# Attention and slot experts in one kernel: zero products, exponentials copied to row groups, logits and row sums moved

## The chip, the cores and the metric

The kernel runs on one core of one Trainium2 chip. The metric is the device time of one execution in microseconds. Six runs of the kernel before gave 151.49 to 153.0 us, with a median of 152.21 us.

## The reference, cut to what matters

Attention over 4 batches, 8 heads, 768 positions and 64 columns a head, with two kinds of mask; its output, as 3072 rows of 512 columns, goes into a layer of 8 experts with 4 slots each. The logits are exponentiated and normalised twice: over the rows (what goes into a slot) and over the 32 slots (what comes back out).

```python
mask = np.where(retr[0, :, 0, 0, None, None], full_mask, stream_mask)
scores = np.where(mask[None, :, :, :], scores, -1000000000.0)
a = np.exp(scores - np.max(scores, axis=-1, keepdims=True))
a = a / (np.sum(a, axis=-1, keepdims=True) + 1e-09)
x = np.matmul(a, v)                  # then (B*S, H*D)
...
logits = x @ phi                     # (3072, 32)
d = np.exp(logits - logits.max(0, keepdims=True))
d /= d.sum(0, keepdims=True) + 1e-09
slot_input = (d.T @ x).reshape(E, S_per_e, D)
for e in range(E):
    h = np.maximum(slot_input[e] @ w1[e], 0.0)
    slot_out[e] = h @ w2[e]
c = np.exp(logits - logits.max(1, keepdims=True))
c /= c.sum(1, keepdims=True) + 1e-09
return c @ slot_out                  # (3072, 512)
```

## The kernel before, in words

The kernel leaves out both subtractions of a maximum, since the values are small, so one exponential of the logits serves both normalisations.

Attention goes through 16 pairs of heads (n), four pairs to a batch (bt counts them, one pair late: bt = 0 to 3 for the pairs 4b+4 to 4b+7). A pair has six groups (g), each a piece of the causal triangle. The order is written out by hand: the loop over n and g issues, on every engine, the score products (qk, L114), the exponentials on ACT (L119, L123), the masks on DVE (L133, L136), the transposes of the next pair's q, k and v (L78) with their evacuations (L91), the products with v (pvmm, L149), the normalisation (norm, L160 and L162) and the transpose of the pair before for the logits (x_transpose, L170, evac_x, L176). Each engine works through its own instructions in this order.

For each batch, three steps follow one or two pairs behind: token_logits multiplies the transposed attention output with phi (L188); exp_tokens takes the exponential (L199) into elg, which has the 32 slots four times side by side, in four groups of columns; exp_slots multiplies elg with a permutation (L205), which brings the slots onto 128 partitions, four copies of each, in expT. dispatch (L219) multiplies the first group of columns of elg with the attention output, to the slots' input. row_sums (L239, L240) sums expT over the slots for each row and takes the reciprocal, which only the last step (piece, L592 and L594) uses. These small results share a PSUM pool of two buffers, "tr", with the transposes.

warm (L62) issues products of zeros into a PSUM tile that is not read. They stand at L333 (20, while the first loads arrive), at L377 (4, after the first transposes), and in the tail.

GpSimd's queue has the loads that also turn float32 into bfloat16: q, k and v of pair n + 3 (L69) and one expert weight of 1024 KB in most pairs (L273), all remaining weights in pair 13 (L275). A load waits until its buffer is free. The queue works in order. Only the first q and k and small inputs go by SP and ACT, and the output goes by SP (L595).

After the last pair comes the tail: logits and exponentials of the last batch, the slots' input (L231), the experts' first layer (L520), transposes, and the second layer (layer2, L548) expert by expert. The weights of experts 6 and 7 for it come in two column halves. slot_cols (L574) scales a half, and piece (L589) makes the output: first the left halves of batches 0 and 1, then their right halves, then whole rows of batches 2 and 3. ACT and DVE evacuate the output products alternately.

Of the kernel before, what the change touches and what calls it, by code (L numbers as in the profile page):

```python
# [14 lines left out]
ACT = mybir.ActivationFunctionType  # L15
# [4 lines left out]
P = 128  # L20
# [15 lines left out]
class Attn:  # L36
# [152 lines left out]
                                      start=first, stop=True, skip_group_check=True)  # L189
                first = False  # L190

    def exp_tokens(self, b, c, groups=range(4)):

        if b not in self.elg:
            self.elg[b] = self.small.tile([P, 6, 4, 32], BF16, tag="eb", name="elg", bufs=1)
        e = self.lg[b, c][:, :, :]
        e = bass.AP(tensor=e.tensor, offset=e.offset,
                    ap=[e.ap[0], e.ap[1], [0, len(groups)], e.ap[2]])
        self.nc.scalar.activation(self.elg[b][:, 3 * c:3 * c + 3, groups[0]:groups[-1] + 1, :], e, ACT.Exp)  # L199

    def exp_slots(self, b, c, eng=None):

# [41 lines left out]
def kernel(  # L244
# [13 lines left out]
    nc = tc.nc  # L258
    B, H, S, D = q.shape
# [11 lines left out]
    def w_load(i, c0=0, cl=DM):  # L271
        if i < NE:
            nc.gpsimd.dma_start(w1s[i], moe_w1[i].rearrange("(di do) f -> di do f", do=4))  # L273
        else:
            nc.gpsimd.dma_start(w2s[i - NE][:, :, c0:c0 + cl],  # L275
                                moe_w2[i - NE].rearrange("(fi fo) d -> fi fo d", fo=8)[:, :, c0:c0 + cl])
# [20 lines left out]
    with ExitStack() as actx:  # L297
# [20 lines left out]
        at = Attn(nc, tc, actx, q, k, v, env)  # L318
# [11 lines left out]
        at.zeros = asing.tile([P, 256], BF16, name="zeros")  # L330
        at.waste = at.pvp.tile([P, 256], F32, tag="pv1", name="waste")
        nc.vector.memset(at.zeros, 0.0)
        at.warm(20)  # L333
        nc.gpsimd.memset(ident, 1.0)
        nc.gpsimd.affine_select(ident, ident, pattern=[[-1, P]], compare_op=ALU.is_equal,
                                fill=0.0, base=0, channel_multiplier=1)
# [37 lines left out]
        cast("k", 1, hi, nc.vector)  # L374
        at.transpose(0, "q")
        at.transpose(0, "k")
        at.warm(4)  # L377
        at.evac(0, "q")
        at.evac(0, "k")

# [4 lines left out]
        def head_mask(h):  # L385
            for c0, c1, r in ((0, 256, r0), (256, 640, r1)):
                nc.vector.tensor_scalar(msk[:, h, c0:c1], level[:, c0:c1], r[:, h:h + 1], 2.0,  # L387
                                        op0=ALU.add, op1=ALU.is_ge)

        for n in range(NP):  # L390
            if n + 3 < NP:
                at.load(n + 3)
            for _ in range(len(w_order) if n == 13 else 0 if n % 4 == 3 else 1):
                if w_order:
                    w_load(*w_order.pop(0))
            if n == 1:

                nc.gpsimd.memset(sum4, 1.0)
                for g in range(4):
                    nc.gpsimd.affine_select(sum4[32 * g:32 * (g + 1)], sum4[32 * g:32 * (g + 1)],  # L400
                                            pattern=[[-1, ES]], compare_op=ALU.is_equal,
                                            fill=0.0, base=0, channel_multiplier=1)
                phf = at.small.tile([P, 4, ES], F32, tag="eb", name="phf", bufs=1)
                nc.sync.dma_start(phf, moe_phi.rearrange("(do di) s -> di do s", di=P))
            for g in range(NG):
                at.qk(n, g)
                last = n == NP - 1

                b, bt = (n - 4) // 4, (n - 4) % 4 if n >= 4 else 0
                if g == 0:  # L410
                    if n == 0:
                        at.transpose(0, "v")
                        head_mask(0)
                        at.evac(0, "v")
                        head_mask(1)


                        nc.vector.tensor_scalar(fb0, r0, 1.0, 30000.0, op0=ALU.subtract, op1=ALU.mult)
                        nc.vector.tensor_scalar(fb1, r1, 1.0, 30000.0, op0=ALU.subtract, op1=ALU.mult)
                    else:  # L420
                        at.pvmm(n - 1, 4)
                        at.v_blocks(n)
                        at.evac_blocks(n)
                    at.mask(n, 0)
                elif g == 1:
                    if n:
                        at.pvmm(n - 1, 5)
                    else:
                        at.v_blocks(n)
                        at.evac_blocks(n)  # L430
                    if bt == 1:
                        at.token_logits(b, 0)
                        at.exp_tokens(b, 0)
                    elif bt == 3:
                        at.dispatch(b, slot_bf if last else None)
                    if n:
                        at.norm(n - 1, 1)
                elif g == 2:
                    if not last:
                        at.transpose(n + 1, "q")  # L440
                    at.pvmm(n, 0)
                    at.mask(n, 1)
                    if not last:
                        at.evac(n + 1, "q")
                elif g == 3:
                    if not last:
                        at.transpose(n + 1, "k")
                    at.pvmm(n, 1)
                    at.mask(n, 2)
                    if not last:  # L450
                        at.evac(n + 1, "k")
                elif g == 4:
                    if not last:
                        at.transpose(n + 1, "v")
                    at.pvmm(n, 2)
                    if bt == 1:
                        at.token_logits(b, 1)
                        at.exp_tokens(b, 1)
                    if bt == 3:
                        at.row_sums(b)  # L460
                    if not last:
                        at.evac(n + 1, "v")
                    if 1 <= bt <= 2:
                        at.exp_slots(b, bt - 1)
                elif g == 5:
                    if n:
                        at.x_transpose(n - 1)
                    at.pvmm(n, 3)
                    if n:
                        at.evac_x(n - 1)  # L470
                    at.norm(n, 0)
                if (n, g) in MASK_AT:
                    head_mask(MASK_AT[n, g])
                if n == 2 and g == 0:
                    nc.vector.tensor_copy(phi, phf)
                if n == 3 and 2 <= g:
                    gg = g - 2
                    for e4 in range(2):
                        s0 = SPE * (4 * e4 + gg)
                        nc.vector.reduce_sum(emask[32 * gg:32 * (gg + 1), e4:e4 + 1],  # L480
                                             sum4[32 * gg:32 * (gg + 1), s0:s0 + SPE], axis=AX.X)
        n, b = NP - 1, B - 1
# [13 lines left out]
        at.waste = at.pvp.tile([P, 256], F32, tag="pv0", name="waste")  # L496
        at.warm(2)
        at.token_logits(b, 0, range(3, 4))
        at.exp_tokens(b, 0, range(1))
        at.warm(4)  # L500
        at.x_transpose(n, range(3, 6))
        at.evac_x(n, range(3, 6))
        at.slots_in(sip, b, range(3))
        at.token_logits(b, 1, range(3, 4))
        at.exp_tokens(b, 1, range(1))
        for c in range(2):
            at.exp_tokens(b, c, range(1, 4))
        at.warm(2)
        at.slots_in(sip, b, range(3, 6))
        nc.vector.tensor_copy(siT, sip)  # L510
# [33 lines left out]
        def layer2(e, c0=0, cl=DM):  # L544
            e4, g = e // 4, e % 4
            for fo in range(8):
                r = fo % 4
                nc.tensor.matmul(sp[32 * r:32 * (r + 1), c0:c0 + cl], hT[e4][:, fo, 32 * g:32 * (g + 1)],  # L548
                                 w2s[e][:, fo, c0:c0 + cl], start=(e == 0 and fo < 4),
                                 stop=(e == NE - 1 and fo >= 4), skip_group_check=True)  # L550
# [16 lines left out]
        h_transpose(1, 1)  # L567
        for e in range(2, NE - 2):
            layer2(e)
        at.row_sums(B - 1)  # L570

        def slot_cols(c):

# [6 lines left out]
        def piece(b, r, m, c0=0, cl=DM):  # L580

            er = expT[:, b, :].rearrange("p (t r) -> p r t", r=6)
            ov = out[b * S:(b + 1) * S, :].rearrange("(p r) d -> p r d", r=6)
            ot, o = ots[2 * b + r // 3], r % 3
            for i in range(m):
                k = count[0] = count[0] + 1
                pool, tag = ((at.scp, "sc"), (at.trp, "tr"))[k % 2]
                op = pool.tile([P, DM], F32, tag=tag, name="op")
                nc.tensor.matmul(op[:, :cl], er[:, r + i, :], slot_out[:, c0:c0 + cl], start=True, stop=True)  # L589
                rr = rrow[:, b, r + i:r + i + 1]  # L590
                if k % 2:
                    nc.scalar.activation(ot[:, o + i, c0:c0 + cl], op[:, :cl], ACT.Copy, scale=rr)  # L592
                else:
                    nc.vector.tensor_scalar_mul(ot[:, o + i, c0:c0 + cl], op[:, :cl], rr)  # L594
            nc.sync.dma_start(ov[:, r:r + m, c0:c0 + cl], ot[:, o:o + m, c0:c0 + cl])  # L595
# [4 lines left out]
        slot_cols(0)  # L600
        for b, r, m in ((0, 0, 1), (0, 1, 2), (0, 3, 3), (1, 0, 3), (1, 3, 3)):
            piece(b, r, m, 0, HALF)
        for e in (NE - 2, NE - 1):
            layer2(e, HALF, HALF)
        slot_cols(1)
# [40 lines left out]
```

The softmax here doesn't subtract the row's maximum and nothing guards it: scores larger than these inputs give would overflow.

## Time and profile before

One profiled execution had a span of 149.8 us and a time of 151.49 us, which is the fastest of the six runs; what lies around the span is 1.7 us.

| | before |
|---|---|
| median of 6 runs | 152.21 us |
| profiled execution, its own time | 151.49 us |
| its span | 149.8 us |
| PE busy | 127.2 us (85%) |
| DVE busy | 115.9 us (77%) |
| ACT busy | 114.2 us (76%) |
| GpSimd busy | 42.9 us (29%) |
| read from HBM, written | 52.50 MB, 6.29 MB |

The busy times are sums over the whole span. The attention loop lasts to about 112 us, the tail's products to 126 us; the last loads land at 132.6 us and the last output at 147.8 us. In the lists below, a line begins with the time at which it starts and its length in us; PE is TensorE, DVE VectorE, ACT ScalarE, POOL GpSimd; a name ending in q is that engine's queue. In brackets stands how long the engine was idle before, and what ended the idle time.

### The profile page before, as it was taken

The numbers are of one execution on the slowest core, as the hardware profiler recorded it, in microseconds if no ns is written. First come the engines' busy times: TensorE is split into PE (matmuls) and PEld (weight loads), VectorE is DVE, ScalarE is ACT, GpSimd is POOL, SyncE is SP. The second block draws the span as 40 slices with busy tenths as digits, with TensorE's granted clock in tenths as the row PEclk, the third lists the DMA queues.
The fourth block names the chain that finished last, engine by engine and source line by source line (L and its number), as shares of the span: only waits on it lengthen the run. The fifth ranks groups of instructions, "written<-read, shape, count | busy, mean of one in ns | idle before, by whom it ended". The sixth has DMA issues, their size and how long they took to land.

```text
span 149.8 us, 5539 instructions
## 1 busy us (share of the span) xinstructions
PE 127.2 (85%) x2372; PEld 85.0 (57%) x2372; DVE 115.9 (77%) x287; ACT 114.2 (76%) x183; POOL 42.9 (29%) x77
## 2 busy tenths in 40 slices
PE   7679899998999999999999999999968997739500
PEld 5446566665776666676666667766556453424100
DVE  6399999899897998989799898979965251528800
ACT  3287989998998998999899889989982431738600
POOL 7865524160541515055141332632000000000000
PEclk9999999999999999999999999999999999996985
DMA  4899999999999999999999999999999999999994
GB/s 119 170 209 205 231 191 222 202 229 196 204 228 195 229 194 222 204 201 225 201 226 199 215 210 200 225 214 221 217 214 214 203 194 199 198 340 319 392 415 203
DMA packets 20663, 33.31 MB, mean 222 GB/s; under 512 B 1952, under 2 KB 17952, under 8 KB 18848
## 3 DMA queue, kind: packets, MB, share of 16 engines
q0 software_dynamic: 15744, 25.83, 94.3%
q1 hardware_dynamic: 4688, 6.76, 12.9%
q10 hardware_dynamic: 208, 0.39, 0.9%
q8 instruction: 18, 0.29, 0.7%
q14 instruction: 5, 0.04, 0.1%
HBM read 52.50 MB, written 6.29 MB: 393 GB/s over the span
## 4 chain that ended last, share of the span: by engine, by line
DMA 34%; DVE 30%; PE 15%; ACT 7%; issue 6%; POOL 2%; DVEq 0%; POOLq 0%; ACTq 0%
DMA w<-in_moe_w_dram 20%; DMA vr<-in_v_dram 10%; DVE xb L162 6%; DVE pT L136 5%; PE pv L149 4%; DVE pT L133 4%; ACT pT L123 4%; DMA w<-in_q_dram 3%; DVE vb L103 3%; PE sc L114 3%; DVE xT L176 3%; PE tpx L170 2%; PE op L589 2%; POOL w L275 2%; DVE msk L387 2%
## 5 line engine op out<-in xcount | busy, mean ns | idle before, releaser
L123 ACT ACTIVATE pT<-sc,fb 128x512 bf16<-128x512 f32 (+1 forms) x96 | 52.2, 621 | 3.5 <-PE sc L114 3.1
L119 ACT ACTIVATE pT<-sc 128x1024 bf16<-128x1024 f32 (+1 forms) x48 | 44.6, 953 | 4.1 <-PE sc L114 3.2
L149 PE MATMUL pv<-vb,pT 128*128 128x65 bf16 x672 | 36.9, 194 | 4.3 <-DVE pT L133 2.3
L114 PE MATMUL sc<-qT,kT 64*128 64x256 bf16 (+3 forms) x320 | 35.0, 281 | 0.3
L149 PEld LDWEIGHTS <-pT 128*128 128x128 bf16 x672 | 26.3, 97 | 15.4 <-issue 6.7
L136 DVE TENSOR_TENSOR pT<-pT,msk 128x1024 bf16<-128x1024 bf16 (+1 forms) x32 | 19.8, 618 | 0.0
L162 DVE TENSOR_TENSOR xb<-pv,rs 128x384 bf16<-128x384 f32 x32 | 17.8, 558 | 1.1
L69 POOL DMA_DIRECT2D qr<-in_q_dram x15 | 9.6, 639 | 27.3 <-PE sc L114 12.7
L114 PEld LDWEIGHTS <-kT 64*128 64x128 bf16 x320 | 10.6, 94 | 7.6 <-issue 1.3
L594 DVE TENSOR_SCALAR w<-op,rrow 128x256 f32<-128x256 f32 (+1 forms) x18 | 9.3, 568 | 6.2 <-PE op L589 6.2
L176 DVE COPY xT<-tpx 128x768 bf16<-128x768 bf16 (+1 forms) x17 | 9.1, 533 | 4.2 <-PE tpx L170 4.1
L69 POOL DMA_DIRECT2D vr<-in_v_dram x16 | 10.4, 647 | 6.7 <-PE tpv L78 4.5
L69 POOL DMA_DIRECT2D kr<-in_k_dram x15 | 9.5, 636 | 5.8 <-issue 1.8
L133 DVE TENSOR_TENSOR pT<-pT,msk 128x1024 bf16<-128x1024 bf16 x16 | 10.9, 682 | 0.0
L275 POOL DMA_DIRECT2D w<-in_moe_w_dram x10 | 6.8, 679 | 13.9 <-DMA w<-in_moe_w_dram 11.8
L589 PE MATMUL op<-slot_out,expT 128*128 128x256 bf16 (+1 forms) x36 | 8.7, 351 | 1.8 <-ACT slot_out L574 1.1
L592 ACT ACTIVATE w<-op,rrow 128x256 f32<-128x256 f32 (+1 forms) x18 | 8.9, 542 | 1.2 <-PE op L589 0.9
L78 PE MATMUL tpq<-ident,qr 96*64 96x96 bf16 x256 | 8.7, 209 | 1.2 <-DVE qr L368 1.2
L91 DVE COPY kT<-tpk 128x768 bf16<-128x768 bf16 x16 | 8.8, 552 | 0.5 <-PE tpk L78 0.5
L170 PE MATMUL tpx<-ident,xb 128*128 128x128 bf16 x96 | 8.2, 220 | 0.9 <-ACT elg L199 0.7
L103 DVE COPY vb<-tpb 128x768 bf16<-128x768 bf16 x16 | 8.9, 557 | 0.0
L91 DVE COPY vT<-tpv 128x768 bf16<-128x768 bf16 x16 | 8.8, 548 | 0.0
(86 smaller groups left out, 158.0 us busy)
## 6 DMA issues: line engine op xcount, KB each, us to landing
w<-in_moe_w_dram POOLq DMA_DIRECT2D x14, 1024.0 KB, 15.4
vr<-in_v_dram POOLq DMA_DIRECT2D x16, 192.0 KB, 11.3
out_dram<-w SPq DMA_DIRECT2D x4, 768.0 KB, 5.6
qr<-in_q_dram POOLq DMA_DIRECT2D x15, 192.0 KB, 11.7
kr<-in_k_dram POOLq DMA_DIRECT2D x15, 192.0 KB, 11.4
out_dram<-w SPq DMA_DIRECT2D x6, 384.0 KB, 4.3
w<-in_moe_w_dram POOLq DMA_DIRECT2D x4, 512.0 KB, 30.5
out_dram<-w SPq DMA_DIRECT2D x2, 256.0 KB, 3.6
```

The source lines that it names most:

```text
L69: self.nc.gpsimd.dma_start(t[:96], self.src[w][b, h:h + 2].rearrange("h (p s) d -> p h (s d)", s=8))
L91: self.nc.vector.tensor_copy(o, i)
L103: self.nc.vector.tensor_copy(self.vbufs[n % 2][:, :, :, :64], tp.rearrange("p (j h d) -> p h j d", j=6, h=2))
L114: nc.tensor.matmul(sc[:, hh, c:c + ni * P], kT[po:po + 64, j * P:(j + 1) * P], qT[po:po + 64, i0 * P:(i0 + ni) * P], start=True, stop=True)
L119: nc.scalar.activation(pT[:, :, :L], sc[:, :, :L], ACT.Exp, scale=self.scale)
L123: nc.scalar.activation(pT[:, hh, :L], sc[:, hh, :L], ACT.Exp, scale=self.scale, bias=fb[:, h + hh:h + hh + 1])
L133: nc.vector.tensor_mul(v, v, m)
L136: nc.vector.tensor_mul(pT[:, :, :L], pT[:, :, :L], self.msk[:, h:h + 2, c:c + L])
L149: self.nc.tensor.matmul(self.pv[n, lo][:, hh, i % 3, :], pT[:, hh, o:o + P], vb[:, hh, j, :65], start=first, stop=True, skip_group_check=True)
L162: nc.vector.tensor_mul(xo, pv[:, :, :, :64], rs.to_broadcast([P, 2, 3, 64]))
L176: self.nc.vector.tensor_copy(self.xT[n // 4][:, n % 4, c], self.tp.pop(("x", n))[:, c])
L589: nc.tensor.matmul(op[:, :cl], er[:, r + i, :], slot_out[:, c0:c0 + cl], start=True, stop=True)
```

## The change

The change has four parts. First, more products of zeros: 27 in place of 20 at the start, 6 in place of 4 after the first transposes, 3 after the transposes of the first v, and 4 at the end of each of the groups 0, 1 and 2 of pair 0. Second, exp_tokens takes the exponential into the first group of columns only, and another engine copies that to the other three: GpSimd for batches 0 and 1, DVE for batches 2 and 3. Third, the logits and exponentials of a batch move from groups 1 and 4 of their pair to the ends of groups 0 and 3, and the two exp_slots move from group 4 of the pairs with bt = 1 and 2 to groups 1 and 4 of the pair with bt = 2. Fourth, the row sums leave the attention loop: those of batches 0 and 1 come before the second layer of the last two experts, those of batches 2 and 3 after the first half of the output pieces.

```diff
-    def exp_tokens(self, b, c, groups=range(4)):
+    def exp_tokens(self, b, c, eng):
 
         if b not in self.elg:
             self.elg[b] = self.small.tile([P, 6, 4, 32], BF16, tag="eb", name="elg", bufs=1)
-        e = self.lg[b, c][:, :, :]
-        e = bass.AP(tensor=e.tensor, offset=e.offset,
-                    ap=[e.ap[0], e.ap[1], [0, len(groups)], e.ap[2]])
-        self.nc.scalar.activation(self.elg[b][:, 3 * c:3 * c + 3, groups[0]:groups[-1] + 1, :], e, ACT.Exp)
+        e = self.elg[b][:, 3 * c:3 * c + 3]
+        self.nc.scalar.activation(e[:, :, 0, :], self.lg[b, c], ACT.Exp)
+        eng.tensor_copy(e[:, :, 1:, :], e[:, :, :1, :].to_broadcast([P, 3, 3, 32]))
...
-        at.warm(20)
+        at.warm(27)
...
-        at.warm(4)
+        at.warm(6)
...
                     if n == 0:
                         at.transpose(0, "v")
+                        at.warm(3)
                         head_mask(0)
...
-                    if bt == 1:
-                        at.token_logits(b, 0)
-                        at.exp_tokens(b, 0)
+                    if bt == 2:
+                        at.exp_slots(b, 0)
                     elif bt == 3:
                         at.dispatch(b, slot_bf if last else None)
...
-                    if bt == 1:
-                        at.token_logits(b, 1)
-                        at.exp_tokens(b, 1)
-                    if bt == 3:
-                        at.row_sums(b)
                     if not last:
                         at.evac(n + 1, "v")
-                    if 1 <= bt <= 2:
-                        at.exp_slots(b, bt - 1)
+                    if bt == 2:
+                        at.exp_slots(b, 1)
...
+                if n == 0 and g < 3:
+                    at.warm(4)
+                if bt == 1 and g in (0, 3):
+                    at.token_logits(b, g // 3)
+                    at.exp_tokens(b, g // 3, nc.vector if b == B - 2 else nc.gpsimd)
...
-        at.exp_tokens(b, 0, range(1))
+        at.exp_tokens(b, 0, nc.vector)
...
-        at.exp_tokens(b, 1, range(1))
-        for c in range(2):
-            at.exp_tokens(b, c, range(1, 4))
+        at.exp_tokens(b, 1, nc.vector)
...
-        at.row_sums(B - 1)
+        for b in range(2):
+            at.row_sums(b)
...
         for b, r, m in ((0, 0, 1), (0, 1, 2), (0, 3, 3), (1, 0, 3), (1, 3, 3)):
             piece(b, r, m, 0, HALF)
+        for b in range(2, B):
+            at.row_sums(b)
         for e in (NE - 2, NE - 1):
             layer2(e, HALF, HALF)
         slot_cols(1)
```

## The prediction

> **What bounds the kernel now.** I read the page's slices first, because a busy share per engine hides which engine is never idle.
>
> ```profile
> DMA  4899999999999999999999999999999999999994
> GB/s 119 170 209 205 231 191 222 202 229 196 204 228 195 229 194 222 204 201 225 201 226 199 215 210 200 225 214 221 217 214 214 203 194 199 198 340 319 392 415 203
> ```
>
> PE, DVE and ACT each reach nine tenths in most slices up to 112 us, but only the DMA engines are full in every slice from the third (7.5 us) to the one before last. The GB/s row counts bytes at the destination. Up to 132 us nearly all of it is float32 read and bfloat16 written, so 200 to 230 there are 400 to 460 read. The page's queue part gives GpSimd's queue q0 25.83 MB written, 51.7 MB read; its packets in the trace run from 4.8 to 132.6 us, so 51.7/127.8 = 404 GB/s over the whole stretch. That is the rate of the end as well, where only output is written (399 to 430 GB/s from 141 to 147 us). A stream with the same rate through all stages of the computation is not paced by it.
>
> Then the chain of waits in order of time:
>
> ```profile
> 42.55 0.48 ACT elg L199
> ...
> 45.89 0.55 ACT elg L199
> ...
> 59.08 0.31 PE rp L239 x6
> 59.41 0.21 DVE rrow L240
> ...
> 79.00 15.51 DMA vr<-in_v_dram
> 94.50 0.28 issue
> ...
> 102.56 30.32 DMA w<-in_moe_w_dram
> 132.92 0.43 PE sp L548 x8
> ```
>
> It runs over the compute engines up to 79 us and over DMA from there. Read literally, the computation released the load of vr at 79.00. But this load has 192 KB, 0.9 us at 210 GB/s, and it took 15.51 us: it stood behind 14.6 us of other loads. Issued sooner it would have stood longer. The GpSimd timeline shows the same from the issuing side:
>
> ```profile
> 41.24 0.56 POOL L273 DMA_DIRECT2D w<-in_moe_w_dram  x1 [0.18 <-issue]
> 43.09 0.64 POOL L69 DMA_DIRECT2D qr<-in_q_dram  x1 [1.29 <-DMA kr<-in_k_dram]
> 44.22 0.64 POOL L69 DMA_DIRECT2D kr<-in_k_dram  x1 [0.49 <-PE tpk L78]
> 45.36 0.63 POOL L69 DMA_DIRECT2D vr<-in_v_dram  x1 [0.50 <-PE tpv L78]
> 49.08 0.56 POOL L273 DMA_DIRECT2D w<-in_moe_w_dram  x1 [3.09 <-DMA w<-in_moe_w_dram]
> ```
>
> Issued minus landed, worked out from these times and the 1024 KB and 192 KB of the issue table, the queue never holds less than 1.68 MB (8 us) after 11 us. Last, the timeline of the tail, where the weights meet the computation:
>
> ```profile
> 125.51 0.44 PE L239 MATMUL rp<-quarter,expT 128*128 128x1 bf16 x6
> ...
> 127.42 0.40 PE L548 MATMUL sp<-w,hT 128*32 128x256 bf16 x8 [1.14 <-DMA w<-in_moe_w_dram]
> ...
> 129.20 13.50 SPq L595 DMA_DIRECT2D out_dram<-w  x14
> ...
> 130.78 0.40 PE L548 MATMUL sp<-w,hT 128*32 128x256 bf16 x8
> 132.92 0.40 PE L548 MATMUL sp<-w,hT 128*32 128x256 bf16 x8 [1.74 <-DMA w<-in_moe_w_dram]
> ```
>
> PE is early twice: 1.14 us for the first column half of the last weights, 1.74 us for the second. From 132.92 only 4.7 MB of output remains. So the end is: loads landed, then output bytes over rate. One hole is left, by the table of stretches:
>
> ```profile
> 134.00:135.00 1.00, 0.77 (x6) 0.58 (x6) 0.68 (x2) 0.80 (x2) 0.00 (x0) 0.68 0.95 333
> 135.00:136.00 1.00, 1.00 (x6) 0.59 (x5) 0.84 (x3) 0.90 (x3) 0.00 (x0) 0.50 0.75 257
> 136.00:137.00 1.00, 1.00 (x6) 0.41 (x5) 0.96 (x3) 0.95 (x3) 0.00 (x0) 0.50 1.03 352
> ```
>
> The last three columns are granted clock, DMA share, GB/s. Against 352 the two rows before it miss 19 + 95 = 114 KB, 0.32 us. PE's clock is at half there.
>
> **What the Trainium skill says.** "DMA: Bandwidth & Descriptors", Where 436 GB/s comes from, puts the ceiling of the 16 engines at 435 GB/s; 404 over 128 us and up to 430 at the end agree with a stream at its limit. "SBUF — State Buffer", Who interferes with whom, says that VectorE and GpSimd share one port pair as an exclusive lock and that a vector instruction with two SBUF inputs blocks against a GpSimd instruction that reads SBUF; the masks (L133, L136) are of that kind. No GpSimd instruction of before reads SBUF beside them, so the trace is silent. "GPSIMD Engine Reference", 3.1 Elementwise, gives 1.03 to 2.6 cycles an element at 1.2 GHz: for 288 elements an estimate of 0.25 to 0.62 us. "TensorE: Matmul & The Clock Gate", What's actually happening, says the clock halves after an idle window of about 3.4 us; the trace agrees, with 0.50 from 134.4 us, after PE had been mostly idle since 131.2.
>
> **The change, part by part.**
> *Products of zeros.* A warm 128x256 product costs about 0.11 us: the four at 114.08 take 0.60, one alone 0.27, so (0.60 - 0.27)/3. The first 20 end at 5.18 and the cast is waited for until 6.38; seven more at 0.11 to 0.2 end at 5.9 to 6.6. I take 5.9, nothing. Two more after the transposes: PE would end at 8.18 instead of 7.97, kT is ready at 8.03: 0.1 us. Then 3 + 3 x 4 = 15 in groups 0 to 2 of pair 0, 1.65 us of PE against waits of 0.41 (vT) and 0.49 (vb). Score products g1 slip from 8.87 to about 9.7, g2 from 10.11 to 10.9, g3 from 11.74 to 12.5. DVE sets this pair (without a gap from 8.61 to 20.09) and its inputs stay just in time until the evacuations at 13.31 and 14.21, which come 0.05 and 0.3 late. On the compute line: between -0.2 (if the clock would otherwise have dropped; it did not here) and +1.9 (all 17 on the path); I take +0.5. The loads freed by these transposes are covered by 5.4 us of queue.
> *Exponentials.* Six ACT instructions of 128x384 (511 ns) become 128x96 (250 ns), and two of 128x288 (412 ns) go: 6 x 0.26 + 0.8 = 2.4 us of ACT, of which 1.06 lies on the chain before 79 us. Four GpSimd copies come for batches 0 and 1, at 0.25 to 0.62 us. Four DVE copies come for batches 2 and 3: the nearest rows are a 128x256 copy (226 ns) and 128x384 (358 ns), so 0.25 to 0.36 each. Those of the tail fit DVE's gaps before 115.06 and 116.64. Readers of the copied columns (L205) come a pair later, readers of the first column (L219) need no copy, so no one waits.
> *GpSimd's queue.* A copy waits for ACT, and three loads stand behind it: q, k, v of pair 9 at 43.09 to 45.36, and of pair 13 at 69.24 to 71.51. With the second copy done at about 45.2 they go at 45.3, 46.2, 47.1; the next weight waits until 49.08 in any case. Cover: 12 us of queue. If it were gone, 2.2 us would show. Cost nothing. DVE behind a held port loses between 0 and 4 x 0.62 = 2.5 us; I take 0.5.
> *Logits moved up.* To groups 0 and 3, the slot products (L205) into the next pair. xT is evacuated at 40.5, the products come at about 41.2: no new wait. The transposes of v in group 4 now wait for the evacuation of k, up to 0.5 us in pairs 5, 9, 13; I take 0.5 in all.
> *Row sums.* Out of pairs 7, 11 and 15: 0.31 of PE and 0.21 of DVE each, about 1.0 us of compute line. Ahead of the first half stand two instead of one, +0.44. The other two stand between the first half's output products and L548 at 130.78: 0.88 against PE's wait of 1.74, so L548 for expert 6 ends at 132.06 and 0.86 is left. The PSUM turns they need are freed by ACT by 131.2.
> *Sum.* Compute line: +0.5 + 0.5 + 0.5 - 1.6 - 1.0 + 0.44 = -0.7 us, so PE waits 1.8 instead of 1.14 at 127.42. Landings unchanged, output unchanged: 0. At most 0.32 us comes back if the added products keep the clock up; I take 0.1. The profiled execution, span 149.8 and 151.49 in all, is the fastest of the six and 0.7 under their median 152.21; taken off the median this gives 152.1.
>
> **Rivals.** *The chain is literal (faster).* If loads are paced by the computation, what it saves before 79 us comes off the end: four exponentials 1.06, one pair of row sums 0.52, 1.6 in all: 150.6. For it: the chain, and GpSimd's waits on PE (12.7 us for qr). Against: 8 us of queue.
> *The clock stays up in the tail.* 0.32 us, 151.9. For it: row sums fall into the idle window. Against: one-column products are little activity.
> *The computation comes too late (slower).* Place: PE at 127.42. All bounds upward: 17 products 1.9, GpSimd holding DVE 2.5, row sums 0.44, 4.8 us with nothing saved. 1.14 is PE's wait. Output then begins after 129.20, which costs nothing while loads remain: q0 moved 1.35 MB after 124 us, 0.99 of it by 129, and 0.36 MB alone at 198 GB/s ends at 130.8. So 1.6 us more is free and the mechanism decides from 2.7 us of delay; at 4.8 the DMA engines idle 2.1 us: 154.3. Against: savings of over 2 us.
>
> **Numbers.** Within 0.5% (0.76 us, what a measurement can tell from no change): my case 0.52, the clock 0.10, in all 0.62. The literal chain 0.19 and other gains 0.03: faster 0.22. Late computation 0.13 and others 0.03: slower 0.16. The range 150.9 to 153.3 takes in the likeliest case's own 151.45 to 152.95, and part of both outer cases, leaving out about 0.2.
>
> **What would show it.** Right: the last loads land within 0.5 us of 132.6; PE's wait at the first half grows past 1.14; q, k, v of pairs 9 and 13 are issued about 2 us later and land no later; row sums end before 132. Wrong: last loads landing over 0.7 us earlier (paced by computation) or output beginning after 130.8.

## The result: 0.14% slower, most of it outside the span

| | before | after |
|---|---|---|
| median | 152.27 us (72 runs) | 152.35 us (35 runs) |
| ratio, with its 95% interval | | 1.0014, 1.0002 to 1.0025 |
| profiled execution, its own time | 151.49 us | 152.08 us |
| its span | 149.8 us | 150.4 us |

The time is within 0.5% of the one before, as forecast, but on the other side of it: the forecast was 0.1 us faster, and the change is 0.2 us slower by the ratio. Two further series gave 1.0020 (0.9999 to 1.0041) and 1.0016 (1.0001 to 1.0031), so the difference is small and real. The two profiled executions differ by more, 0.6 us of span, but they don't show it. The spans of the kernel before run from 149.5 to 151.7 us in 211 executions of the experiments, with a mean of 150.47; the profile before had caught one of the shortest. 72 executions of the kernel after have a mean span of 150.52. Standard errors are 0.02 and 0.04, so the spans are equal within what can be told. Executions more than 1.5% above the fastest of their kernel, five of all, are left out of these counts and of those below.

What differs is the time around the span, an execution's time less its span. Before it is 1.71 us in the mean and at most 1.79; after it is 1.91 in the mean and goes up to 2.95. These 0.2 us are most of the measured slowdown: over the same executions the mean time grew by 0.25 us, and the 0.05 us left are in the span and about one standard error of the difference. A span is recorded to 0.1 us, so the time around it is known to 0.05 us for one execution, and better for a mean. The experiments were made to find the cause.

### The profile page after: what moved, and what is told of

It reads as the page before. It is cut to its first block, busy times and chain, and to the rows that moved or that the text cites. A ratio compares the mean times of both kernels' runs of the same rounds, so it can differ in the third digit from the quotient of the medians.

```text
span 150.4 us, 5599 instructions
## 1 busy us (share of the span) xinstructions
PE 131.1 (87%) x2396; PEld 87.4 (58%) x2396; DVE 117.0 (78%) x291; ACT 113.6 (76%) x181; POOL 44.9 (30%) x81
## 4 chain that ended last, share of the span: by engine, by line
PE 31%; DMA 30%; DVE 24%; issue 5%; POOL 2%; ACT 2%; DVEq 0%; POOLq 0%
DMA w<-in_moe_w_dram 20%; DMA vr<-in_v_dram 10%; PE pv L149 7%; PE sc L114 6%; DVE xb L162 6%; PE waste L62 5%; DVE pT L136 4%; DVE pT L133 3%; PE tpv L78 3%; DVE vb L103 3%; PE op L587 3%; DVE xT L176 3%; PE tpx L170 2%; POOL w L274 2%; DVE w L592 2%
## 5 line engine op out<-in xcount | busy, mean ns | idle before, releaser
L62 PE MATMUL waste<-zeros 128*128 128x256 bf16 x58 | 10.2, 330 | 1.1 <-DVE zeros L331 1.1
L587 PE MATMUL op<-slot_out,expT 128*128 128x256 bf16 (+1 forms) x36 | 9.6, 395 | 1.4 <-ACT slot_out L572 1.1
L78 PEld LDWEIGHTS <-vr 96*64 96x64 bf16 x256 | 6.6, 109 | 3.4 <-issue 3.4
```

What stands on the lines that cost most here:

```text
L62: self.nc.tensor.matmul(self.waste[:, :cols], self.zeros[:, :P], self.zeros[:, :cols], start=True, stop=True)
```

## The profile after

The page's slices and queues first: the DMA engines are as full as before, and the queues carry the same packets.

```profile
DMA  4899999999999999999999999999999999999994
...
q0 software_dynamic: 15744, 25.83, 93.9%
...
q8 instruction: 18, 0.29, 0.7%
```

q8 brings instructions: 18 packets, 16 KB each. The forecast made no use of this row, which is the same before the change.

The end of the chain of waits (start, length, what) has the shape of before:

```profile
79.49 14.97 DMA vr<-in_v_dram
...
102.61 30.82 DMA w<-in_moe_w_dram
133.47 0.43 PE sp L545 x8
```

GpSimd's timeline shows the two copies in front of the loads of pair 9:

```profile
41.36 0.57 POOL L272 DMA_DIRECT2D w<-in_moe_w_dram  x1 [0.18 <-issue]
42.80 0.71 POOL L198 COPY elg<-elg 128x288 bf16<-128x288 bf16 x1 [0.87 <-ACT elg L197]
45.85 0.43 POOL L198 COPY elg<-elg 128x288 bf16<-128x288 bf16 x1 [2.34 <-ACT elg L197]
46.36 0.65 POOL L69 DMA_DIRECT2D qr<-in_q_dram  x1
47.00 0.64 POOL L69 DMA_DIRECT2D kr<-in_k_dram  x1
47.63 0.63 POOL L69 DMA_DIRECT2D vr<-in_v_dram  x1
49.29 0.56 POOL L272 DMA_DIRECT2D w<-in_moe_w_dram  x1 [1.02 <-DMA w<-in_moe_w_dram]
```

The load of q leaves 3.3 us later than before (46.36 against 43.09), the next weight 0.2 us later. The stream did not slow down for it: by the packets of q0 in the trace, the tenth million bytes had landed at 54.97 us (before: 54.86; over all profiles 54.86 to 55.06) and the twenty-fifth at 126.84 (before: 126.70). Over all kernels of this study, the twenty-fifth million lands between 126.70 and 127.00 us.

The tail of the timeline, the row sums and the last two experts:

```profile
125.57 0.72 PE L238 MATMUL rp<-quarter,expT 128*128 128x1 bf16 x12
...
126.22 0.40 PE L545 MATMUL sp<-w,hT 128*32 128x256 bf16 x8
128.22 0.40 PE L545 MATMUL sp<-w,hT 128*32 128x256 bf16 x8 [1.59 <-DMA w<-in_moe_w_dram]
...
130.10 13.19 SPq L593 DMA_DIRECT2D out_dram<-w  x14
131.99 0.85 PE L238 MATMUL rp<-quarter,expT 128*128 128x1 bf16 x12
...
132.78 0.40 PE L545 MATMUL sp<-w,hT 128*32 128x256 bf16 x8
...
133.47 0.40 PE L545 MATMUL sp<-w,hT 128*32 128x256 bf16 x8 [0.30 <-DMA w<-in_moe_w_dram]
```

PE is early at both halves of the last weights, as before. The first half came at 128.22 instead of 127.42 and the output began 0.9 us later. While it was missing, the DMA engines ran short (the last columns are clock, DMA share, GB/s):

```profile
129.00:130.00 1.00, 0.81 (x4) 0.58 (x4) 0.19 (x1) 0.54 (x2) 0.00 (x0) 0.50 1.21 164
130.00:131.00 1.00, 1.00 (x5) 0.50 (x4) 0.96 (x3) 0.97 (x4) 0.00 (x0) 0.50 0.83 117
131.00:132.00 1.00, 1.00 (x6) 0.50 (x5) 0.96 (x3) 0.98 (x4) 0.00 (x0) 0.50 1.18 263
```

That looked like the cause, and was the first theory to be tried. But the landing of the first half, with PE already waiting for it, was at 127.45 in another profile of the kernel before, and at 127.81 to 128.90 in kernels with only a part of the change or none of it. It belongs to the single execution.

## The experiments

Theory 1 is the forecast's: loads landed, then output bytes over rate, and no part matters. Theory 2: output that begins later costs, since the engines run dry one by one from 129 us; the half clock of PE belongs to it. Theory 3: the computation reaches the end. Theory 4: GpSimd's copies hold up the loads. Theories 5 and 6 came up on the way: the number of instructions. In the table, "products" is the number of PE's products on the run's page (each is two instructions, a weight load and the product), "around" is time less span, and "over 1.80" counts executions in which that is over 1.80 us. The kernel before has 2372 products, 0 of 211 over 1.80.

| run | products | executions | mean span | mean around (largest) | over 1.80 | ratio (95%) |
|---|---|---|---|---|---|---|
| the change, three series | 2396 | 72 | 150.52 | 1.91 (2.95) | 33 | 1.0014, 1.0020, 1.0016 |
| only_products | 2396 | 21 | 150.37 | 2.00 (3.03) | 11 | 1.0013 (0.9994 to 1.0032) |
| only_rows | 2372 | 14 | 150.42 | 1.71 (1.76) | 0 | 1.0003 (0.9986 to 1.0019) |
| only_exps | 2372 | 22 | 150.45 | 1.71 (1.76) | 0 | 1.0006 (0.9990 to 1.0022) |
| no_masks | 2372 | 20 | 150.38 | 1.71 (1.79) | 0 | 0.9998 (0.9988 to 1.0009) |
| late2 | 2390 | 20 | 150.37 | 1.72 (1.78) | 0 | 0.9986 (0.9970 to 1.0003) |
| late4 | 2408 | 4 | 153.15 | 1.76 (1.81) | 1 | 1.0181 (1.0132 to 1.0230) |
| fill_tail | 2418 | 22 | 150.95 | 1.72 (1.83) | 2 | 1.0029 (1.0017 to 1.0041) |
| fill_swap | 2394 | 21 | 150.49 | 1.76 (2.05) | 6 | 1.0002 (0.9984 to 1.0020) |
| extra_end | 2418 | 5 | 152.14 | 1.75 (1.84) | 1 | 1.0116 (1.0101 to 1.0131) |
| same_before | 2372 | 14 | 150.59 | 1.71 (1.75) | 0 | 1.0008 (0.9992 to 1.0025) |
| before_end24 | 2396 | 22 | 150.50 | 1.80 (2.66) | 6 | 1.0013 (0.9998 to 1.0029) |
| after_less12 | 2384 | 22 | 150.58 | 1.70 (1.77) | 0 | 1.0010 (0.9994 to 1.0026) |

### The change and its three parts

again is the changed kernel without an edit. only_products is the kernel before with the products of zeros:

```diff
-        at.warm(20)
+        at.warm(27)
...
-        at.warm(4)
+        at.warm(6)
...
                         at.transpose(0, "v")
+                        at.warm(3)
...
+                if n == 0 and g < 3:
+                    at.warm(4)
```

only_rows has the edits of row_sums, and only_exps those of exp_tokens, token_logits and exp_slots, as the change's diff shows them.

> The changed kernel once more, as the yardstick for its three parts on the same chip. Theory 1 (the forecast's: loads landed, then output bytes over rate; no part matters): ratio 1.000, within 0.001. Theory 2 (the drain: in the profile of the changed kernel output begins at 130.10 instead of 129.20 while DMA engines already run dry, 117 GB/s at 130 to 131 us): ratio 1.001 to 1.0025 again.

> The kernel before with the 24 added products of zeros alone. Theory 1 and theory 2: ratio 1.000 within 0.001, since the attention loop is covered by the queue of loads; its loads of pair 4 leave about 0.7 us later and land no later. Theory 3 (the added products delay the first pair and that reaches the end): 0.7 us, ratio 1.004.

> The kernel before with the row sums moved alone. Theory 1: 1.000 within 0.001. Theory 2: PE comes to the first half of the last weights with one more pair of row sums but about 0.5 us earlier, waits longer, its clock halves, the first output is issued later than 129.2 us: ratio 1.001 to 1.0025, the whole of the difference.

> The kernel before with exponentials taken once, copied by GpSimd and DVE, and the logits and slot products moved, alone. Theory 1 and theory 2: 1.000 within 0.001; three loads of pairs 9 and 13 leave GpSimd about 3 us later and land no later. Theory 4 (GpSimd's copies in front of the loads cost the stream): the last loads land over 0.3 us later, ratio 1.002.

Measured: no part stands clear of 1 by itself. Theory 2 wanted all of the difference in the row sums (1.0003), theory 3 wanted 1.004 for the products, theory 4 wanted later loads from only_exps; none came. The ratios could not decide more. The split of each time into span and the rest did: the products have the long time around the span, and the other two parts don't have it in a single execution.

### Does the computation pace the loads at all, and when is output late?

no_masks is the kernel before with this on the three calls of mask, so it leaves the masks out from pair 2 on:

```diff
-                    at.mask(n, 0)
+                    if n < 2:
+                        at.mask(n, 0)
```

> The kernel before without the multiplications by the masks (L133, L136) from pair 2 on: 42 DVE instructions of 550 to 690 ns, about 27 us of DVE, are left out, so the output is that of unmasked attention inside the groups. Theory 1 (the stream of loads paces the kernel): the last loads land within 0.3 us of 132.9, ratio 1.000 within 0.003. Theory 3 (the literal chain: the computation paces the loads): DVE pieces of L133 and L136 make 8.3% of the chain, over 8 us before the load of 79 us; ratio 0.95 or less.

Measured: 0.9998. DVE is busy 75.8 of the 100 us from 10 to 110, before 93.7, and PE comes to its row sums 2.2 us earlier, only to wait. PE's timeline of no_masks:

```profile
123.32 0.44 PE L239 MATMUL rp<-quarter,expT 128*128 128x1 bf16 x6
125.85 0.40 PE L551 MATMUL sp<-w,hT 128*32 128x256 bf16 x8 [2.10 <-DMA w<-in_moe_w_dram]
128.13 0.62 PE L551 MATMUL sp<-w,hT 128*32 128x256 bf16 x8 [1.88 <-DMA w<-in_moe_w_dram]
...
133.41 0.40 PE L551 MATMUL sp<-w,hT 128*32 128x256 bf16 x8 [0.64 <-DMA w<-in_moe_w_dram]
```

Of the four groups of products of the last two experts, three wait for their weights, and the last one starts at 133.41 us, no earlier than with the masks (132.92 in the profile before, 133.24 in same_before). DVE's busy time over the whole span is 20.4 us less, and the time is the same. The literal chain is refuted.

late2 and late4 put products behind the row sums of the tail of the kernel before (18, then 36):

```diff
         at.row_sums(B - 1)
+        at.warm(18)
```

> The kernel before with 18 products of zeros, about 2 us of PE, in front of the second layer of the last two experts. Forecast's step: delays up to 2.7 us are free, ratio 1.000. Theory 2 (the engines run dry one by one from 129 us, so output that begins later costs from the first tenth): output begins about 0.9 us later than before, ratio 1.001 to 1.003.

> The same with 36 products, about 4 us of PE: output begins at about 132. Forecast's step: 1.3 us over the free 2.7, ratio 1.008. Theory 2: 2.9 us late and most of it lost, ratio 1.012 to 1.018.

Measured: the 18 products cost nothing (0.9986), and the 36 cost 1.81%, 2.7 us. So products in PE's wait are free up to a point, as the forecast said. Where the point lies is not shown. The forecast's 1.3 us of loss for late4 compares with 2.7 us, but late4 also has a 19th instruction packet, of which more below. Its output ends with three packets of 6 KB, one after the other, 0.7 us in all, as in fill_tail below. Without them, 2.0 us are left in the mean, and 1.5 us in the profiled execution (span 152.7). Four executions, with spans of 152.1 to 154.1 us, can't tell this from 1.3.

Nor is theory 2 refuted as a mechanism. late2 is a weak test of it: its output began at 130.37 us, later than the 129.20 of the short profile before, but hardly later than in most profiles. Over the 13 profiled executions with 18 packets in the span, the later the output begins, the longer the span (correlation 0.85, about 0.6 us for 1 us): 129.20 and 149.8 before, 129.24 and 150.1 in same_before, 130.10 and 150.4 after, 130.68 and 150.9 in only_exps. Whether the late start is the cause, or both follow from late weights, no run separates. It is a difference between single executions, and not one between the two kernels, whose mean spans agree.

### Keeping PE's clock up

fill_tail puts products into PE's waits of the changed kernel's tail:

```diff
         for e in (NE - 2, NE - 1):
             layer2(e, 0, HALF)
+            at.warm(10 if e == NE - 2 else 3)
...
             layer2(e, HALF, HALF)
+            at.warm(6 if e == NE - 2 else 3)
```

> The changed kernel with products of zeros in PE's waits of the tail: 10 and 3 around the last expert's first half, 6 and 3 around its second half. Theory 1: 1.0015, as the changed kernel. Theory 2: PE's clock stays at full until after the first output pieces, output runs on sooner, ratio 0.998 to 1.000.

Measured: the clock stayed at full to 145.1 us, and the kernel got slower, 1.0029. Its page and the last 6 us of its DMA (146 to 152, GB/s in 40 slices) show why:

```profile
q8 instruction: 19, 0.31, 0.7%
```

```profile
GB/s 532 369 369 451 369 492 410 369 492 369 451 451 287 492 410 369 164 82 41 0 41 41 0 0 0 0 0 0 0 0 0 0 0 0 0 0 0 0 0 0
```

There is one instruction packet more. In the window from 136 to 138 us it takes 2.9% of 16 engines, 0.029 x 16 x 2 = 0.93 us of one engine. At the end, the output no longer stops at once: after 148.5 us a few packets come one at a time. Up to 6.2 MB of output the fill_tail kernel is level with the changed kernel (148.51 against 148.40 us), and the last 0.09 MB takes it 0.98 us instead of 0.35. The last three packets of 6 KB take 0.24 us each, and each starts as the one before it ends. I read this as one engine that had the instructions to fetch and is behind with its share; the records don't name the engine.

fill_swap has the same filled waits, but not the products of the first pair, so it has 2 products fewer than the changed kernel. extra_end is the changed kernel with 22 products behind everything:

```diff
         for b in range(2, B):
             for r in (0, 3):
                 piece(b, r, 3)
+        at.warm(22)
```

> The changed kernel without its products in the first pair, but with 22 in PE's waits of the tail: 4 instruction rows fewer than the changed kernel. Theory 5: 18 packets, and the loss of the earlier kernel with filled waits (1.0029) is gone. Theory 2 (PE's half clock in the tail costs): clock full until the output products end, span 150.2 or less, ratio below 0.999. If the clock costs nothing: span 150.4 to 150.5, ratio 1.000.

> The changed kernel with 22 more products of zeros behind the last output product, where PE has nothing left to do. Theory 5 (instructions are fetched in pieces of 16384 bytes over the same DMA engines; 44 more instruction rows bring a 19th piece in the tail, which holds one engine 0.9 us): 19 packets in the instruction queue, span 0.3 to 0.5 us above the changed kernel's 150.5, ratio about 1.004. Theory 1: as the changed kernel, 1.0015 or less.

Measured: with 18 packets the loss of the filled waits is gone (1.0002), and so is the case for the clock: at full clock until PE's last product, fill_swap's span is 150.49 us, that of before 150.47. Its table of stretches shows why (clock, DMA share and GB/s are last):

```profile
135.00:136.00 1.00, 0.77 (x6) 0.48 (x5) 0.97 (x3) 1.00 (x3) 0.00 (x0) 1.00 0.88 311
136.00:137.00 1.00, 0.95 (x6) 0.58 (x5) 1.00 (x3) 1.00 (x4) 0.00 (x0) 1.00 0.73 243
```

The hole in the output that the forecast laid to PE's half clock (333 and 257 GB/s from 134 to 136 us) is there at full clock too, and so is the other one: 116 GB/s from 130 to 131 us, 117 in the changed kernel at half clock.

With 22 products where PE has no other work, the 19th packet is back and costs 1.16%, more than theory 5 had said. extra_end's last 6 us:

```profile
GB/s 573 205 492 328 369 574 328 369 614 287 410 492 246 532 410 328 573 123 0 41 41 0 41 41 0 41 41 0 0 0 0 0 0 0 0 0 0 0 0 0
```

The packets that come singly go on to 150.3 us, 1.6 us behind the rest. The products themselves don't cost this: before_end24, below, has 24 at the same place, 18 packets, and a span of 150.50.

### The number of instructions, or their place?

same_before is the kernel before and again2 the changed kernel, both without an edit.

> The kernel before against itself: how far a ratio strays with nothing changed. Ratio 1.000; if it lies 0.001 or more off, the difference of the changed kernel (1.0014) is no more than that.

> The changed kernel a third time. If the difference of 1.0014 is real: 1.0005 to 1.0025. If it was chance: 0.999 to 1.001, and mean spans of both kernels within 0.1 us.

Measured: 1.0008 for nothing, with an interval that holds 1, and 1.0016 for the change once more. The profile of again2 caught what happens. Its DMA from 150 to 153 us, after the last output (149.0 us):

```profile
GB/s 0 0 0 0 0 0 0 0 0 0 0 0 0 0 0 0 0 0 0 0 218 0 0 0 0 0 0 0 0 0 0 0 0 0 0 0 0 0 0 0
...
q8 instruction: 1, 0.02, 2.7%
```

One packet of instructions, 0.027 x 16 x 3 = 1.3 us long, at the very end, and this execution's time is 1.94 us over its span. Five more profiles of kernels with 2394 or 2396 products, with times of 1.68 to 1.82 us over their spans, show no such packet. The next two kernels separate the number of products from their place: before_end24 is the kernel before with at.warm(24) where extra_end has its 22; after_less12 is the changed kernel with warm(20), warm(4) and none after the transposes of v, but with the 4 in groups 0 to 2.

> The kernel before with the change's 24 products placed behind the last output product, where PE has nothing left to do. Theory 6 (the number of instructions, not their place: 48 more rows put PE's closing instructions into another piece of the program, which some executions fetch after the output is written): span unchanged at 150.4 to 150.5, but what lies around the span grows from 1.71 to a mean of 1.85 to 2.0, with single executions over 2.1; ratio 1.001 to 1.002. Rival (the products cost by their place in the first pair): around the span 1.71 in every execution, ratio 1.000.

> The changed kernel with 12 of its 24 added products taken out again (20, 4 and none, the 4 in groups 0 to 2 stay): 24 rows fewer. Theory 6: around the span 1.71 in every execution, span 150.4 to 150.5, ratio 0.9995 to 1.0007. Rival (the changed kernel is slower for another reason): around the span 1.85 or more, ratio 1.001 or more.

Measured: before_end24 has the long times around the span (6 of 22, up to 2.66), at a place where the products delay nothing. after_less12, with half the products still in the first pair, has none (largest 1.77). So it is the number that brings the long times. The mean of before_end24, 1.80, is short of the 1.85 to 2.0 that was expected, and the share of long times differs between the kernels that have them (6 of 22 to 11 of 21); what sets it is open. Over all runs, up to 2390 products, 0 of 323 executions are over 1.80 us; at 2394 and 2396, 56 of 136 are; from 2408 on, the 19th packet is inside the span and makes that longer instead.

The pages' counts of the instructions of all engines part the kernels at the same place (up to 5575, 5587 to 5599, from 5611). The packets tell whose count it is. For the kernel before, PE and its weight loads (the first two counts) from 13 to 127 us, and q8 in the same window:

```profile
13.00:127.00 114.00, 107.75 (x2172) 73.36 (x2169) 97.26 (x233) 98.06 (x156) 33.81 (x57) 1.00 1.13 211
...
q8 instruction: 18, 0.29, 0.9%
```

From the first of these packets (13.2 us) to the last (126.5) that is one for every 255 of PE's instructions, so q8 feeds PE's queue. Behind the 18th packet PE has 123 to 159 instructions left in the profiles of the kernels without long times, and 171 to 185 in those with them; in late4, fill_tail and extra_end the 19th packet starts after 178 to 194. The edge lies where the next packet falls due.

No version here beat the kernel before: with the stream of loads fixed, the only lasting effects found are losses. after_less12's ratio, 1.0010, cannot be told from 1 or from the change's own.

## Why the prediction was wrong, point by point

**The step that failed** is the products of zeros. The forecast priced them as time on PE alone ("seven more at 0.11 to 0.2 ... I take 5.9, nothing"; +0.5 us of the compute line in all, which doesn't reach the end) and, in the sum, took the time around the span as fixed when it subtracted from the median. The 24 products are also 48 instructions, and these take the program over an edge beyond which the time around the span is long in some executions. The forecast had no term for that; it measured 0.2 us in the mean. That the products do it is shown by only_products, before_end24 and after_less12; that it is one more packet of instructions at the end is seen in one trace.

**The 0.1 us that was to come back** with the clock did not: fill_swap had the clock, and the hole in the output stayed. Its ratio alone, with 0.2% either way, could not exclude 0.1 us. Without that term the forecast would have been 152.2, no change, and the sign would still have been open.

**What bounds the kernel** was right, and the runs show it: no_masks takes 20 us of DVE's busy time out and changes the time by 0.02%. The literal chain, given 0.19, is refuted. The last load landed at 133.16 us, 0.6 later than in the profile before and just outside the forecast's own mark of 0.5; same_before, without an edit, has 132.93.

**The compute line** was wrong where it did not matter. It was to come to the tail's row sums 1.1 us earlier (the -0.7 of the sum less the 0.44 of the row sums there) and came 0.06 later (125.57 against 125.51). The first pair cost 0.65 (the load of q of pair 4 left at 12.09 instead of 11.44; +0.5 was taken), and this was made good by 38.6 us. The savings of 1.6 and 1.0 do not appear; where they went was not followed, since PE waits for weights in either case.

**GpSimd's queue**: copies of 0.43 to 0.71 us (estimate 0.25 to 0.62), q of pair 9 at 46.36 (45.3 was said), the cover held. DVE lost next to nothing: the masks take 617 and 685 ns in the mean, before 618 and 682. Only two of the four copies ran beside a mask. At 42.80 us the copy began second and took 0.71 us instead of 0.43, the mask 0.68 as elsewhere; at 69.62 the mask began second and took 0.74 instead of 0.68. The 0.5 us that was taken for DVE came to some 0.06. DVE's own copies of 0.26 us came out as estimated.

**Row sums**: the slack of 0.86 us before the second half was 0.30, as output began later and PE ran at half clock (0.85 us for 12 products instead of 0.72). The row sums ended at 132.8 us, not before 132. The slack was 0.20 to 0.32 in the profiles of only_rows, again, again2 and extra_end, and none is seen in that of after_less12. only_rows shows no cost.

**The late computation**, given 0.13, did not occur in the mean, and its price is not settled: late2 was free, late4 lost 1.5 to 2.0 us where 1.3 was forecast, on four executions. The forecast let the loads of q0 run out evenly, so that a later output would cost nothing until 130.8 us; the table of stretches above shows 117 GB/s at 130 us, and single executions whose output begins later are longer.

## What to carry to other kernels

Where a stream of loads is full from start to end, ask of each edit only what it does to the stream, to the first and last transfers, and to the size of the program. Instructions that fill an engine's waits are not free for being hidden: they are fetched by DMA beside the data, and here one packet more cost 0.5 us where the filled waits brought nothing. To see a tenth of a per cent, split each time into span and remainder, and look at the distribution: here the medians could not separate the parts, while 33 of 72 executions against 0 of 211 did at once.

## What the runs showed of the hardware that was not expected

Instructions come in packets of 16 KB, 0.93 us for one in the middle of the output and 1.3 us for one after it. The Trainium skill, "Advanced Engine Details and Errata", ISA Cache, gives a cache line of 16 KB, 256 instructions. The packet size agrees, and so do the 255 of PE's instructions to a packet. The edge that was met here lies between 2390 and 2394 products, where a 19th packet falls due. That the packet at the end is what lengthens these executions rests on the one trace that shows it, the five without it, and the count; which executions fetch it and which don't is open. A 19th packet inside the span went with 0.48 us (fill_tail) or 1.67 us (extra_end) over the mean span of before. It came at 136 to 138 us in the one and at 141.4 in the other; that this is the reason for the difference was not tested.

The stream of loads is steadier than the kernel: its twenty-fifth million bytes lands within 0.3 us of each other in all profiles of the study, while the first half of the last weights, 1 to 2 us later, lands anywhere from 127.4 to 128.9 us in single profiles.
